# Local attention output transposed by DMA instead of TensorE, with the first layer's products issued one at a time

## The chip, the cores and the metric

The kernel runs on one core of one Trainium2 chip. The metric is the device time of one execution in microseconds (us). A core has TensorE (PE in the profile, with its weight loads as PEld), VectorE (DVE), ScalarE (ACT), GpSimd (POOL) and SyncE (SP); each works through its own instructions in the order in which the kernel issues them, and they wait for one another by semaphores. Loads are issued from POOL, stores and DMA transposes from SP.

## What is computed

Sparse attention over 8 batches, 8 heads, 576 positions and head dimension 64, and after it a two-layer perceptron on 4608 tokens (512 to 2048 to 512) with the Mish function between. Heads 0 to 3 are local (a position sees the 32 positions up to itself), heads 4 to 7 strided (it sees earlier positions that are congruent to it modulo 32).

```python
rel = pos[:, None] - pos[None, :]
mask_local = (rel >= 0) & (rel < stride)
mask_strided = (rel >= 0) & (pos[None, :] % stride == pos[:, None] % stride)
scores = np.where(masks, scale * q @ k.T, -1e9)
attn = softmax(scores)
x = (attn @ v).transpose(0, 2, 1, 3).reshape(B * S, H * D)
h = x @ w_in
g = h * np.tanh(np.log1p(np.exp(h)))     # Mish
out = g @ w_out
```

## The kernel before

**Blocks.** `run(plan, t)` (L712) is called for t = 1 to 8, after a hand-written start for the first tokens. Block t does three things at once: the first layer for tokens 512t to 512t+511 (`Mlp1(t)`), the second layer for the block before (`Mlp2(t - 1)`, from t = 2), and the attention of batch b = t + 1, as long as b < 8. So attention ends with t = 6; blocks 7 and 8 have none. After them the second layer of the last block remains.

**The layers.** Both are Strassen-like: seven products of half-size matrices in place of eight, with sums of operands formed by DVE ahead of them. In `Mlp1`, the 2048 columns of w_in are four quarter groups g = 0 to 3; each has products 1 to 7 of four matmuls each (`prod`, L386). Their results lie in three PSUM banks be, al and E (of two sets that take turns):

- step a (L411): product 5 into E, copy of E to s5, product 1 into al, copy of al to be by ACT;
- step b: product 6 onto al, copy of al to s2, product 3 onto E, DVE adds E and s2 into h, product 2 onto be;
- step c: product 7 onto al, DVE adds al and s5 into h; step d: product 4 onto al;
- steps U, W, H: Mish on ACT of be, al and h into gT.

The copies to s5 and s2 go to `self.eng`: ACT for t up to 6, DVE for t = 7 and 8. In `Mlp2`, "m" in a plan is one half of a product, eight matmuls (`half`, L470); there are 14. `x_sum` (x0 to x3) and `g_sum` (g1 to g3, and n for the next block) are the DVE sums of the operands; x0 reads the strided rows of xT, x1 to x3 the local ones (x_half, L366).

**Attention.** `qk` (q0 to q5) multiplies transposed q and k and takes the exponential on ACT into P_s and P_l; `mask` multiplies them with a mask, on POOL from t = 3 (in t = 2 the first four on DVE). Each "v" in a plan takes the next of a list: for batches 3 to 7 this is five `pv` of strided heads (s0 to s4), two `xt` of them, then two `pv` of local heads, an `xt`, two `pv`, an `xt`. A `pv` is a few matmuls into bank A0 or A1, a reciprocal and a product on DVE into x_s or x_l. An `xt` (L324) transposes x_s or x_l on PE into one of these banks and copies it into xT, the first layer's operand. xT is a ring of four batches.

**Queues.** "D" issues four DMA transposes of the next batch's raw k and q on SP (kTs, qTs, kTl, qTl; L188); SP also issues the stores of the output. "R" (L790) is on POOL: `hold` reads a corner of each of these four tiles, so that POOL waits until the transposes have landed; then it loads v of the next batch (L154, L157) and q and k of the batch after it (L137, L151). The masks are on POOL too. "s" spreads the loaded v on DVE.

**Order.** The plans are strings, written out, one token to a step; `SECOND` is for t = 1, `MAIN2` for t = 2, `MAIN` for t = 3 to 6 and `PLAIN` for t = 7 and 8. Their order is the order of issue on every engine.

Of the kernel before, what the change touches and what calls it, by code (L numbers as in the profile page):

```python
# [16 lines left out]
NW = 6  # L17
WQ = 96
# [3 lines left out]
RING = 4  # L22
# [23 lines left out]
def kernel(ctx, tc, q, k, v, moe_w_in, moe_w_out, out):  # L46
# [191 lines left out]
    class Attn:  # L238
# [54 lines left out]
        def pv(self, kind, n0, n1, bank, eng=None):  # L293
# [27 lines left out]
                in1=rden[0:m, 0:nu].unsqueeze(2).to_broadcast([m, nu, D]), op=ALU.mult,  # L321
            )

        def xt(self, kind, hf, bank, eng):  # L324
            tr = bank[:].bitcast(BF16)
            t0 = (self.b % RING) * S
            if kind == "l":
                for w in range(NW):
                    u = 12 * hf + 2 * w
                    PE.transpose(  # L330
                        tr[:, WQ * w:WQ * w + WQ], x_l[0:WQ, u:u + 2, :].rearrange("p u d -> p (u d)"),
                        ident[0:WQ, 0:WQ],
                    )
                cast(eng, xT[:, hf, t0:t0 + S], tr[:, 0:S])
            else:
                for j in range(CS):
                    u = 16 * hf + 2 * j
                    PE.transpose(  # L338
                        tr[:, PN * j:PN * j + PN], x_s[0:PN, u:u + 2, :].rearrange("p u d -> p (u d)"),
                        ident[0:PN, 0:PN],  # L340
                    )
                cast(
                    eng, xT[:, 2 + hf, t0:t0 + S].rearrange("p (n j) -> p n j", j=CS),
                    tr[:, 0:576].rearrange("p (j n) -> p n j", j=CS),
                )
# [35 lines left out]
    class Mlp1:  # L381
# [18 lines left out]
                    )  # L400

        def step(self, s, g):
            z = (self.t + g + 1) % 2
            be, al, E = [x[:] for x in SETS[z]]
            if self.eng is Dv:
                z = ((self.t + 1) % 2, 2, self.t % 2, (self.t + 1) % 2)[g]
                be, al, E = [x[:] for x in ((A1, A0, SETS[(self.t + 1) % 2][2]) if g == 1 else SETS[z])]
            h = hh[z]
            o = gT[:, 4 * g:4 * g + 4, :]
            two = lambda x: x.rearrange("p (u n) -> p u n", u=2)  # L410
            if s == "a":  # L411
                self.prod(5, g, E, True)
                cast(self.eng, s5[z][:], E)
                self.prod(1, g, al, True)
                Sc.copy(be, al)  # L415
            elif s == "b":
                self.prod(6, g, al, False)
                cast(self.eng, s2[z][:], al)
                self.prod(3, g, E, False)
                add(Dv, h[:, 0, :], E, s2[z][:])  # L420
                self.prod(2, g, be, False)
            elif s == "c":
                self.prod(7, g, al, False)
                add(Dv, h[:, 1, :], al, s5[z][:])
            elif s == "d":
                self.prod(4, g, al, False)
            elif s == "H":
                Sc.activation(  # L428
                    o[:, :, 256:512], h[:].rearrange("p i (u n) -> p (i u) n", u=2), AF.Mish
                )  # L430
            elif s == "U":
                Sc.activation(o[:, 0:2, 0:256], two(be), AF.Mish)
            elif s == "W":
                Sc.activation(o[:, 2:4, 0:256], two(al), AF.Mish)  # L434
# [130 lines left out]
    with tc.manual_schedule():  # L565
# [146 lines left out]
        def run(plan, t):  # L712
            b = t + 1
            m1, m2, nxt = Mlp1(t), Mlp2(t - 1), Mlp2(t)
            at = Attn(b) if b < B else None
            if b == B:
                unread(1, A1)
            ms = m2.steps() if t > 1 else []
            bank = [1, 0] if t == 1 else [0, 1]

            def v_steps():
                def pv(kind, r):
                    at.pv(kind, *r, (A0, A1)[bank[0]])
                    bank[0] = (bank[0] + bank[1]) % 2

                def xt(kind, hf):
                    at.xt(kind, hf, (A0, A1)[bank[0]], Sc if t == 1 and kind == "l" else Dv)
                    bank[0] = (bank[0] + bank[1]) % 2
                P = lambda kd, r: (lambda: pv(kd, r))
                X = lambda kd, hf: (lambda: xt(kd, hf))  # L730
                if t == 1:
                    return (
                        [P("l", r) for r in PV_L[:3]] + [X("l", 0), P("l", PV_L[3]), P("s", PV_S[0]), X("l", 1)]
                        + [P("s", r) for r in PV_S[1:]] + [X("s", 0), X("s", 1)]
                    )
                return (
                    [P("s", r) for r in PV_S] + [X("s", 0), X("s", 1)]
                    + [P("l", r) for r in PV_L[:2]] + [X("l", 0)]
                    + [P("l", r) for r in PV_L[2:]] + [X("l", 1)]
                )  # L740
            vs_ = late + (v_steps() if at else [])
            late.clear()
            JOBS = [("s", 0), ("s", 1), ("s", 2), ("l", 0), ("l", 1), ("l", 2)]
            for w in plan.split():
                c, n = w[0], int(w[1:]) if len(w) > 1 else 0
                if c in "abcdHUW":
                    m1.step(c, n)
                elif c == "p":
                    plain(t, n, deal1[n], act=False)
                elif c == "y":  # L750
                    Sc.activation(gT[:, n, :], deal1[n][:], AF.Mish)
                    if deal1[n] is A0:
                        bank[:] = [0, 1]
                elif c == "w":
                    w_out_sums(n, Dv)
                elif c == "m":
                    ms.pop(0)()
                elif c == "x":
                    x_sum(t, n, Dv)
                elif c == "g":  # L760
                    m2.g_sum(n, Dv)
                elif c == "n":
                    nxt.g_sum(0, Dv, 0, 8)
                elif not at:
                    continue
                elif c == "e":
                    Sc.preload_act_table(AF.Exp)
                elif c == "f":
                    Sc.preload_act_table(AF.Mish)
                elif c == "q":  # L770
                    at.qk(*JOBS[n], PAIRS[n % 2 * (1 + (t + 1) % 2)])
                    at.mask(*JOBS[n], Dv if t == 1 or t == 2 and n in (0, 1, 2, 3) else Po)
                elif c == "v":
                    if vs_:
                        vs_.pop(0)()
                elif c == "s":
                    spread_v(Dv)
                    if t > 1:
                        share_v(b, Dv)
                elif c == "h":  # L780
                    share_v(b, Dv)
                elif b + 1 >= B:
                    continue
                elif c == "t":
                    t_step(2, "l", "kq"[n // 2], n % 2, (C[1], C[2], A0, A1)[n], (Sc, Dv)[n % 2])
                    if n == 3:
                        load_qk(3)
                elif c == "D":
                    transpose_by_dma()
                elif c == "R":  # L790
                    hold(kTs, qTs, *((kTl, qTl) if t > 1 else ()))
                    load_vs(b + 1)
                    load_vl(b + 1)
                    if b + 2 < B:
                        load_qk(b + 2)
            assert not ms
            if t == 1:
                late.extend(vs_)
            else:
                for w in vs_:  # L800
                    w()

        late = []
        MAIN = (
            "x0 m m e m m x1 s x2 g1 g2 q0 q1 m m m m g3 q2 q3 m m q4 q5 m D v m f R a0 v v m m v v b0 a1 x3 c0 v "
            "U0 v b1 d0 U1 W0 c1 v a2 d1 W1 v H0 a3 v v b2 v H1 c2 b3 c3 d2 W2 v H3 d3 n U2 U3 W3 H2"
        )
        SECOND = (
            "t0 p0 q2 p1 t1 t2 t3 w1 p2 q3 w2 p3 q5 q4 p4 h p5 p6 f v y0 D y1 p7 s v p8 R y3 y6 v y2 v p9 v v y5 y4 "
            "p10 p11 y9 p12 y8 y7 y11 v v p13 v y13 p14 y10 p15 y14 n v y12 w3 y15"  # L810
        )
        MAIN2 = (
            "v m m v m e v x0 x1 m x2 g1 q1 q0 g2 m m m m g3 q2 s q3 m m q4 q5 m D f v m v a0 R v m m v v b0 a1 x3 "
            "c0 v v b1 d0 U0 U1 W0 c1 v a2 d1 W1 v H0 a3 v v b2 v c2 H1 b3 c3 d2 W2 v H3 d3 U2 U3 W3 H2 n"
        )
        PLAIN = (
            "m m x0 g1 x1 m m x2 x3 a0 m m g2 m b0 m m m g3 m m c0 U0 a1 H0 m m b1 d0 W0 a2 c1 a3 b2 b3 c3 d1 U2 H1 "
            "W1 U1 c2 d3 W3 U3 d2 H2 W2 H3 n"
        )

        for t in range(1, NBLK):
# [40 lines left out]
```

## Time and profile before

| | |
|---|---|
| median of 3 runs | 294.25 us (293.95 to 294.44) |
| the profiled execution | 294.54 us, of it 292.8 us in the span of the profile |
| granted TensorE clock | 0.999 of full speed |
| PE busy per block, t = 3 to 6 | 29.2 to 29.3 of 29.6 to 29.7 us |
| DVE, ACT, POOL busy in such a block (t = 4) | 22.6, 24.4, 17.5 us |
| PE busy, t = 7 | 25.1 of 25.2 us |
| x_l on PE in one block | 12 transposes |

The profile lists, per engine and group of equal instructions, the busy time, the mean duration and the idle time before them with the instruction that ended it. In the timeline, a line gives the start, the duration, the engine, the line of the kernel, the operation, what it writes and reads, and in brackets idle time of that engine just before. The chain of waits is followed back from the last instruction and names at each step what released it. Matmuls are pipelined: each is shown for about 0.27 us, and they start 0.11 us apart.

### The profile page before, as it was taken

Reading aid. Unit: us, or ns where it says so; the run is one execution under the profiler, and the core shown is the slowest. Engines: PE = TensorE matmul, PEld = TensorE weight load, DVE = VectorE, ACT = ScalarE, POOL = GpSimd, SP = SyncE. Lnnn points to the kernel's source line nnn. Section 1 sums busy time; section 2 is a strip of 40 time slices with the busy share of each in tenths; the row PEclk is TensorE's granted clock in tenths of the full one; section 3 lists DMA queues with packets and bytes.
Section 4 is the critical chain, followed back from the end, with each engine's and each line's share of the span. In section 5 each row is a group of like instructions: output and inputs, shape, how many; then the busy total and the mean of one; then the engine's idle time right before and its main releaser. Section 6 shows DMA issues by size and latency. Waiting matters only on the chain.

```text
span 292.8 us, 7799 instructions
## 1 busy us (share of the span) xinstructions
PE 282.4 (96%) x3256; PEld 223.8 (76%) x3268; DVE 205.7 (70%) x387; ACT 204.7 (70%) x361; POOL 102.7 (35%) x109
## 2 busy tenths in 40 slices
PE   8889999999999999999999999999999999999995
PEld 3564545545788888888888888888898888888884
DVE  2583548587798896688768866886688667757842
ACT  2578793769667789778977898789878526825650
POOL 8754330131614533981399039502920000000000
PEclk9999999999999999999999999999999999999999
DMA  7999999999999999999699989950110003003004
GB/s 136 179 204 202 203 194 185 174 169 150 137 154 181 204 174 70 165 223 166 32 167 215 167 39 147 231 36 2 72 73 2 2 29 118 1 3 143 2 0 143
DMA packets 94415, 35.84 MB, mean 122 GB/s; under 512 B 75804, under 2 KB 90124, under 8 KB 94380
## 3 DMA queue, kind: packets, MB, share of 16 engines
q0 software_dynamic: 61712, 18.71, 70.1%
q1 hardware_dynamic: 31708, 15.73, 24.4%
q10 hardware_dynamic: 960, 0.91, 1.0%
q8 instruction: 25, 0.41, 0.6%
q14 instruction: 10, 0.08, 0.1%
HBM read 37.87 MB, written 9.44 MB: 162 GB/s over the span
## 4 chain that ended last, share of the span: by engine, by line
PE 77%; ACT 8%; DVE 7%; issue 3%; DMA 3%; POOL 1%; ACTq 0%; POOLq 0%
PE al L129 34%; PE ee L129 19%; PE be L129 12%; PE at L129 5%; DVE hh L123 4%; PE at L310 3%; ACT s L118 3%; DMA vraw<-in_v_dram 3%; ACT gT L428 1%; PE at L338 1%; ACT Pl L281 1%; ACT gT L434 1%; DVE x_l L319 1%; ACT be L415 1%; PE at L330 1%
## 5 line engine op out<-in xcount | busy, mean ns | idle before, releaser
L129 PEld LDWEIGHTS <-w_in 128*128 128x128 bf16 x464 | 44.3, 98 | 20.6 <-issue 5.0
L129 PEld LDWEIGHTS <-gs 128*128 128x128 bf16 x512 | 48.7, 98 | 6.3 <-DVE gs L123 0.3
L129 PEld LDWEIGHTS <-wis 128*128 128x128 bf16 x472 | 44.5, 99 | 9.2 <-issue 3.2
L129 PEld LDWEIGHTS <-gT 128*128 128x128 bf16 x448 | 42.0, 98 | 10.0
L287 POOL TENSOR_TENSOR Ps<-Ps,consts_sb 72x864 bf16<-72x864 bf16 (+1 forms) x12 | 23.2, 1957 | 48.2 <-ACT Ps L281 48.2
L123 DVE TENSOR_TENSOR gs<-gT,gs 128x2048 bf16<-128x2048 bf16 x16 | 21.0, 1312 | 15.4 <-PE al L129 9.7
L129 PE MATMUL al<-wos,gs 128*128 128x256 bf16 x256 | 31.8, 273 | 0.0
L129 PE MATMUL al<-xs,wis 128*128 128x256 bf16 x208 | 30.4, 272 | 0.1
L428 ACT ACTIVATE gT<-hh 128x1024 bf16<-128x1024 f32 x26 | 27.7, 1067 | 0.0
L129 PE MATMUL al<-xT,w_in 128*128 128x256 bf16 (+1 forms) x141 | 25.8, 300 | 1.6 <-ACT gT L434 0.9
L129 PE MATMUL be<-xT,w_in 128*128 128x256 bf16 (+1 forms) x139 | 25.1, 299 | 0.2 <-issue 0.2
L287 POOL TENSOR_TENSOR Pl<-Pl,consts_sb 128x960 bf16<-128x960 bf16 (+1 forms) x14 | 22.2, 1608 | 7.6 <-ACT Pl L281 7.6
L129 PE MATMUL be<-w_out,gT 128*128 128x256 bf16 (+1 forms) x157 | 23.3, 293 | 0.2
L314 DVE RECIPROCAL rden<-at 96x6 f32<-96x6 f32 (+2 forms) x64 | 12.1, 189 | 14.6 <-PE at L310 10.8
L434 ACT ACTIVATE gT<-al 128x512 bf16<-128x512 f32 x26 | 15.6, 601 | 7.8 <-PE al L129 7.8
L319 DVE TENSOR_TENSOR x_s<-at,rden 72x448 bf16<-72x448 f32 (+1 forms) x34 | 19.9, 585 | 1.2
L123 DVE TENSOR_TENSOR hh<-al,s 128x512 f32<-128x512 f32 x26 | 17.8, 684 | 2.8 <-PE al L129 2.4
L123 DVE TENSOR_TENSOR hh<-ee,s 128x512 f32<-128x512 f32 x26 | 17.8, 684 | 2.5 <-ACT s L118 1.9
L123 DVE TENSOR_TENSOR gs<-gT 128x2048 bf16<-128x2048 bf16 x16 | 19.5, 1218 | 0.0
L129 PE MATMUL al<-w_out,gT 128*128 128x256 bf16 (+1 forms) x143 | 19.3, 284 | 0.1
L120 DVE COPY xT<-at 128x576 bf16<-128x576 bf16 x25 | 14.5, 597 | 4.5 <-PE at L330 4.3
L319 DVE TENSOR_TENSOR x_l<-at,rden 96x384 bf16<-96x384 f32 x30 | 16.6, 553 | 1.0
(185 smaller groups left out, 573.9 us busy)
## 6 DMA issues: line engine op xcount, KB each, us to landing
out_dram<-osb SPq DMA_DIRECT2D x16, 512.0 KB, 3.4
vraw<-in_v_dram POOLq DMA_DIRECT2D x8, 288.0 KB, 6.1
w_out<-in_moe_w_out_dram POOLq DMA_DIRECT2D x4, 512.0 KB, 15.4
ql<-in_q_dram POOLq DMA_DIRECT2D x7, 288.0 KB, 10.8
vl<-in_v_dram POOLq DMA_DIRECT2D x7, 288.0 KB, 9.1
kl<-in_k_dram POOLq DMA_DIRECT2D x5, 384.0 KB, 11.0
ks<-in_k_dram POOLq DMA_DIRECT2D x6, 288.0 KB, 8.2
qs<-in_q_dram POOLq DMA_DIRECT2D x6, 288.0 KB, 9.1
```

The source lines that it names most:

```text
L118: Sc.copy(out_, in_)
L120: eng.tensor_copy(out_, in_)
L123: eng.tensor_tensor(out=out_, in0=a, in1=b, op=op)
L129: PE.matmul(o, lhsT=lhsT, rhs=rhs, start=start, stop=stop, skip_group_check=True)
L281: Sc.activation(pt[0:n, e, 0:o], ps[e][0:n, 0:o], AF.Exp, scale=scale)
L287: meng.tensor_tensor(out=pm, in0=pm, in1=mk[0:n, :].unsqueeze(1).unsqueeze(1).to_broadcast([n, 2, nu, w]), op=ALU.mult,)
L310: PE.matmul(po[:, n - n0, :], lhsT=pt[0:r, c0:c0 + 128], rhs=rhs, start=True, stop=True)
L314: Dv.reciprocal(rden[0:m, 0:nu], po[0:m, :, D])
L319: Dv.tensor_tensor(out=x[0:m, n0:n1, :], in0=po[0:m, :, 0:D], in1=rden[0:m, 0:nu].unsqueeze(2).to_broadcast([m, nu, D]), op=ALU.mult,)
L330: PE.transpose(tr[:, WQ * w:WQ * w + WQ], x_l[0:WQ, u:u + 2, :].rearrange("p u d -> p (u d)"), ident[0:WQ, 0:WQ],)
L428: Sc.activation(o[:, :, 256:512], h[:].rearrange("p i (u n) -> p (i u) n", u=2), AF.Mish)
L434: Sc.activation(o[:, 2:4, 0:256], two(al), AF.Mish)
```

## The change

Local x of batches 3 to 7 is transposed by two DMA transposes on SP, `xt_by_dma`, each issued right behind the `pv` that completes its half of x_l; the transposes on PE and the copies on DVE for them are gone. "v" has 11 steps in place of 13. "R" is split: V holds on the four transposes and loads v, and R, now at the end of the block, holds on the second half of xT and then loads q and k. Steps a and b are split, so that each product is a step: a, i, b, j, k. A and B are a and b with the copy on the other of the two engines ACT and DVE. The four plans are written anew.

```diff
--- before.py
+++ after.py
@@ -321,6 +321,13 @@
                 in1=rden[0:m, 0:nu].unsqueeze(2).to_broadcast([m, nu, D]), op=ALU.mult,
             )
 
+        def xt_by_dma(self, hf):
+            t0 = (self.b % RING) * S
+            nc.sync.dma_start_transpose(
+                xT[:, hf, t0:t0 + S].rearrange("c (w n) -> c w n", w=NW),
+                x_l[0:WQ, 12 * hf:12 * hf + 12, :].rearrange("p u d -> p (u d)"),
+            )
+
         def xt(self, kind, hf, bank, eng):
             tr = bank[:].bitcast(BF16)
             t0 = (self.b % RING) * S
@@ -400,6 +407,9 @@
                     )
 
         def step(self, s, g):
+            eng = self.eng
+            if s in "AB":
+                s, eng = s.lower(), Dv if eng is Sc else Sc
             z = (self.t + g + 1) % 2
             be, al, E = [x[:] for x in SETS[z]]
             if self.eng is Dv:
@@ -410,14 +420,17 @@
             two = lambda x: x.rearrange("p (u n) -> p u n", u=2)
             if s == "a":
                 self.prod(5, g, E, True)
-                cast(self.eng, s5[z][:], E)
+                cast(eng, s5[z][:], E)
+            elif s == "i":
                 self.prod(1, g, al, True)
                 Sc.copy(be, al)
             elif s == "b":
                 self.prod(6, g, al, False)
-                cast(self.eng, s2[z][:], al)
+                cast(eng, s2[z][:], al)
+            elif s == "j":
                 self.prod(3, g, E, False)
                 add(Dv, h[:, 0, :], E, s2[z][:])
+            elif s == "k":
                 self.prod(2, g, be, False)
             elif s == "c":
                 self.prod(7, g, al, False)
@@ -726,6 +739,10 @@
                 def xt(kind, hf):
                     at.xt(kind, hf, (A0, A1)[bank[0]], Sc if t == 1 and kind == "l" else Dv)
                     bank[0] = (bank[0] + bank[1]) % 2
+
+                def last_l(hf):
+                    pv("l", PV_L[2 * hf + 1])
+                    at.xt_by_dma(hf)
                 P = lambda kd, r: (lambda: pv(kd, r))
                 X = lambda kd, hf: (lambda: xt(kd, hf))
                 if t == 1:
@@ -735,15 +752,14 @@
                     )
                 return (
                     [P("s", r) for r in PV_S] + [X("s", 0), X("s", 1)]
-                    + [P("l", r) for r in PV_L[:2]] + [X("l", 0)]
-                    + [P("l", r) for r in PV_L[2:]] + [X("l", 1)]
+                    + [w for hf in range(2) for w in (P("l", PV_L[2 * hf]), lambda hf=hf: last_l(hf))]
                 )
             vs_ = late + (v_steps() if at else [])
             late.clear()
             JOBS = [("s", 0), ("s", 1), ("s", 2), ("l", 0), ("l", 1), ("l", 2)]
             for w in plan.split():
                 c, n = w[0], int(w[1:]) if len(w) > 1 else 0
-                if c in "abcdHUW":
+                if c in "ABabcdijkHUW":
                     m1.step(c, n)
                 elif c == "p":
                     plain(t, n, deal1[n], act=False)
@@ -787,12 +803,14 @@
                         load_qk(3)
                 elif c == "D":
                     transpose_by_dma()
-                elif c == "R":
+                elif c == "V":
                     hold(kTs, qTs, *((kTl, qTl) if t > 1 else ()))
                     load_vs(b + 1)
                     load_vl(b + 1)
-                    if b + 2 < B:
-                        load_qk(b + 2)
+                elif c == "R" and b + 2 < B:
+                    if t > 1:
+                        hold(xT[:, 1, b % RING * S:])
+                    load_qk(b + 2)
             assert not ms
             if t == 1:
                 late.extend(vs_)
@@ -802,20 +820,22 @@
 
         late = []
         MAIN = (
-            "x0 m m e m m x1 s x2 g1 g2 q0 q1 m m m m g3 q2 q3 m m q4 q5 m D v m f R a0 v v m m v v b0 a1 x3 c0 v "
-            "U0 v b1 d0 U1 W0 c1 v a2 d1 W1 v H0 a3 v v b2 v H1 c2 b3 c3 d2 W2 v H3 d3 n U2 U3 W3 H2"
+            "m m g1 g2 m e m q0 q1 m s m m m q2 q3 g3 m m q4 q5 D m f x0 x1 v V x2 m v a0 v i0 m v m v b0 v a1 i1 j0 "
+            "k0 x3 c0 v b1 j1 d0 U0 c1 k1 W0 A2 U1 i2 v d1 v W1 H0 A3 i3 v v b2 j2 b3 k2 H1 c2 c3 k3 d2 n W2 H2 j3 U3 "
+            "U2 d3 H3 W3 R"
         )
         SECOND = (
-            "t0 p0 q2 p1 t1 t2 t3 w1 p2 q3 w2 p3 q5 q4 p4 h p5 p6 f v y0 D y1 p7 s v p8 R y3 y6 v y2 v p9 v v y5 y4 "
+            "t0 p0 q2 p1 t1 t2 t3 w1 p2 q3 w2 p3 q5 q4 p4 h p5 p6 f v y0 D y1 p7 s v p8 V R y3 y6 v y2 v p9 v v y5 y4 "
             "p10 p11 y9 p12 y8 y7 y11 v v p13 v y13 p14 y10 p15 y14 n v y12 w3 y15"
         )
         MAIN2 = (
-            "v m m v m e v x0 x1 m x2 g1 q1 q0 g2 m m m m g3 q2 s q3 m m q4 q5 m D f v m v a0 R v m m v v b0 a1 x3 "
-            "c0 v v b1 d0 U0 U1 W0 c1 v a2 d1 W1 v H0 a3 v v b2 v c2 H1 b3 c3 d2 W2 v H3 d3 U2 U3 W3 H2 n"
+            "v m m v m e v g1 m q1 g2 q0 s m m m m g3 x0 x1 q3 m q2 x2 m q5 q4 m v D f m v A0 v i0 m V v m v B0 x3 k0 "
+            "A1 i1 c0 v j0 v b1 j1 k1 d0 U0 W0 U1 c1 v a2 i2 d1 v W1 H0 A3 v i3 v b2 j2 k2 H1 c2 b3 j3 k3 c3 d2 d3 W2 "
+            "H3 U2 U3 H2 W3 n R"
         )
         PLAIN = (
-            "m m x0 g1 x1 m m x2 x3 a0 m m g2 m b0 m m m g3 m m c0 U0 a1 H0 m m b1 d0 W0 a2 c1 a3 b2 b3 c3 d1 U2 H1 "
-            "W1 U1 c2 d3 W3 U3 d2 H2 W2 H3 n"
+            "x0 m g1 m m g2 x1 m x2 a0 x3 m i0 m m B0 j0 m m g3 c0 m m m k0 A1 i1 m b1 U0 m d0 W0 j1 H0 a2 i2 c1 k1 "
+            "A3 i3 b2 j2 B3 j3 k3 c3 H1 k2 U1 c2 d1 U2 d3 W1 W3 n d2 H2 H3 W2 U3"
         )
 
         for t in range(1, NBLK):
```

## The prediction

> **What bounds the kernel now.** I read the page's busy shares first, then the block lengths from the timeline (where product 1 of the second layer starts: 107.76, 137.36, 166.95, 196.63, 226.44, 251.64, 276.83 us), then the timeline and the chain of waits inside one block.
>
> ```profile
> PE 282.4 (96%) x3256; PEld 223.8 (76%) x3268; DVE 205.7 (70%) x387; ACT 204.7 (70%) x361; POOL 102.7 (35%) x109
> ```
>
> PE is busy 96% of the span, so TensorE is the bound on average; blocks with attention (t = 3 to 6) take 29.6 to 29.8 us, the two without (t = 7, 8) 25.2 us. Time in a block is counted below from its product 1 (136.9 for t = 4). From the chain: 16 products of 256 columns stream in 1.75 us (0.109 each). A block has 224 of them, 24.5 us; qk adds about 1.34, the PV of strided heads 0.97 and of local heads 4 x 0.18, the transposes of x_s 0.52, those of x_l 0.52. That is 28.57 of 29.6: **0.52 us is local transposes and 1.03 us is loose**. The tail of the block shows both:
>
> ```profile
> 160.89 0.60 PE L129 MATMUL al<-xT,w_in 128*128 128x256 bf16 x4 [0.19 <-ACT gT L434]
> 161.32 0.42 PE L330 MATMUL at<-consts_sb,x_l 96*128 96x96 bf16 x6
> 161.58 0.35 PE L310 MATMUL at<-vl,Pl 128*128 128x65 bf16 x6
> ...
> 165.93 0.42 PE L330 MATMUL at<-consts_sb,x_l 96*128 96x96 bf16 x6
> 166.52 0.60 PE L129 MATMUL al<-xs,w_in 128*128 128x256 bf16 x4 [0.17 <-DVE hh L123]
> ```
>
> A group of six transposes holds PE from 161.32 to 161.58, 0.26 us. In brackets are PE's two marked gaps of the block: once it waits for ACT's Mish, once for DVE's addition. The chain of waits agrees: until 159.2 it is PE throughout, then it runs over ACT and DVE to the end of the block.
>
> ```profile
> 158.77 0.45 PE ee L129 x4
> ...
> 159.25 0.45 ACT s L118
> ...
> 160.24 0.59 ACT gT L434
> 160.84 0.70 ACT gT L428
> ...
> 165.19 1.29 DVE hh L123 x2
> ```
>
> From 159.2 to 166.5 (7.3 us) PE's own work is 13 products, 3 PVs and two transpose groups: 5.69 + 0.54 + 0.52 = 6.75. So this tail is shared by PE, ACT and DVE with only 0.55 us between them.
>
> **The change, part by part.**
>
> *Transposes gone from PE.* Two groups in each of five batches: 10 x 0.26 = 2.6 us of PE's queue, with no cover anywhere, since PE is the bound. Between 0 (if the tail is set by ACT and DVE alone) and 2.6; I take all of it, because the same edit relieves those two engines.
>
> *Casts gone from DVE.* Two copies of 0.46 (rows at 161.78 and 166.39) per batch. Nothing waits for them but the next block, so by themselves 0; they free DVE in the tail.
>
> *Casts moved between ACT and DVE.* In t = 3 to 6, A2 and A3 put two copies of E on DVE (0.68 busy) instead of ACT (0.58, spaced 0.475 when back to back). ACT gains 0.95 us in the tail, DVE takes 1.2 and lost 0.9. I walked the new order by hand with the spacing of the trace (product 0.4375, result 0.16 later; copies 0.475, H 0.94, additions 0.60, rden with x_l 0.70). Positions in the block: a0 at 12.6, b0 15.9, c0 18.3, d0 19.9, d1 22.3, b2 24.1, d2 27.2, d3 28.0, end 28.5. DVE's additions for c2 and c3 come out at 27.1 and 27.7, just ahead of d2 and d3; ACT's W1 at 23.35, about 0.1 after i3 wants its bank. ACT then has 3.2 us of Mish left for the next block; before, H ended 3.5 us in (139.41 + 1.07). So the loose 1.03 falls to some 0.6 (the changes between qk and products, about 0.1 each, stay). Bounds for this part, per block: gain 1.03 (nothing loose left), loss 0.9 (DVE works from 21.8 to the end without a pause; one addition of 0.68 and the spacing after it more in the way). I take 0.33 gained, near the walk.
>
> *t = 2.* The same 0.52; but A0, A1 and B0 also go to DVE, which is busiest there (26.25 of 29.7 us), 3 x 0.69 more against 0.92 less. I take 0.6 in all, with 0 and 1.4 as ends.
>
> *t = 7, 8.* No attention, so no transposes; only the order. 25.2 against 24.5 of products: 0.7 loose, of which one wait for DVE of 0.17 and 0.26. The new order puts d1 and d3 between c2 and d2, so that c2's addition (result 0.16, addition 0.68) has 0.875 us of cover. I take 0.2 per block; ends 0.6 gained, 0.5 lost.
>
> *Ten DMA transposes on SP's queue.* The nearest row is qTl, 96 rows and twice the columns:
>
> ```profile
> 151.31 1.59 SPq L197 DMA_TRANSPOSE qTl<-ql  x1
> ...
> 152.94 1.32 SPq L537 DMA_DIRECT2D out_dram<-osb  x2
> ```
>
> SP holds 1.27 to 1.79 us for one and it lands 3.7 to 7.2 us after issue, median 4.2. For half the data I take 1 and 3.5 (ends 0 and 7.2). Behind them on SP is only the next block's work. Their result is read by x1, x2 of the next block, which moved behind q5 to about 11 us: x_l is ready at 25.9, xT at 29.4, some 10 us early. PE pays 0.
>
> *Loads of q and k behind them.* This is the added wait: on POOL, the hold on xT sits ahead of four loads and these ahead of the next block's masks.
>
> ```profile
> 143.86 5.80 POOL L287 TENSOR_TENSOR Ps<-Ps,consts_sb 72x864 bf16<-72x864 bf16 x3 [11.37 <-ACT Ps L281]
> 149.63 4.83 POOL L287 TENSOR_TENSOR Pl<-Pl,consts_sb 128x960 bf16<-128x960 bf16 x3
> ...
> 157.67 0.73 POOL L137 DMA_DIRECT2D ks<-in_k_dram  x1
> 158.39 0.72 POOL L137 DMA_DIRECT2D qs<-in_q_dram  x1
> 159.10 1.46 POOL L151 DMA_DIRECT2D kl<-in_k_dram  x1
> 160.53 1.22 POOL L151 DMA_DIRECT2D ql<-in_q_dram  x1
> ```
>
> POOL spends 4.1 us on the four; 11.4 us idle ahead of the masks is the cover. With xT landed at 29.4 (0.9 into the next block) and 0.5 for the hold, they are out at 5.5; the first mask wants POOL at 6.5 to 7. Cost 0, with about 1 us in hand. It happens only ahead of t = 3, 4 and 5. The loads land 8 to 12 us after issue, so kTl's transposes start at some 13 us instead of 12 (148.95), the loads of v go out near 19 to 20 and land by 28; the spreading of v is wanted at 5 of the next block. Cost 0.
>
> **Sum**, against the profiled execution of 294.54 us (span 292.8): 4 blocks x (0.52 + 0.33) = 3.4; t = 2 0.6; t = 7, 8 0.4; together 4.4. All up to 77.4 us and the last block are unchanged. That gives 290.1; the median of the runs shown is 0.3 lower, 294.25, so **289.9 us** is the forecast for the median.
>
> **Rivals.**
>
> *Slower: the masks wait for the transposes.* If xT lands after about 30.4 (4.5 us after x_l), POOL's four loads push the masks, and PV s1, which the new order puts at 12.4 us and which needs the third mask (6.5 + 5.8 = 12.3), stops PE one for one. With an SP issue of 3.45 (qTs at 88.33, beside loads) and a landing of 7.2 it would be some 4 us late; half-way, 2.5 us in three blocks: 289.9 + 7.5 = 297.4. For it: v's loads may run beside these transposes, and PE has no slack at s1. Against: with the loads beside them the four transposes at 86.9 took 11.2 us to the last hold, without 9.6, and these are half as large. The Trainium skill, "VectorE: DVE Perf Modes", The three transpose paths and Rules for kernel authors, speaks against the edit: 1309 ns for a 128x128 by DMA, 390 ns on TensorE, which it prefers where PSUM will do; six tiles would be 7.9 us (an estimate from that page), and this rival. The traces bear it out poorly: qTl, twelve tiles, landed in 4.2 us at the median.
>
> *No change: the tail is set by ACT and DVE.* The chain's last 7 us speak for it: PE would wait where it transposed, and the moved casts only shift the queue to DVE. Then the tail stays 7.3 us, and what DVE loses in t = 2 takes what t = 7, 8 give: 292.5 to 294.9.
>
> *More than forecast.* Everything loose closes: 5 x 0.52 + 5 x 0.8 + 2 x 0.5 = 7.6, 286.7.
>
> **How the numbers follow.** Forecast 0.58 (287.9 to 291.8), more 0.05, no gain or little 0.20 (of it 0.08 faster by over 0.2%, 0.05 within, 0.07 slower), masks late 0.17. Within 0.2% (0.6 us) is about what a measurement of this kernel can't tell from no change. Faster 0.71, same 0.05, slower 0.24. The range 287.9 to 295.0 leaves out the 0.05 below and most of the late masks.
>
> **What would show it.** Right: blocks of t = 3 to 6 at 28.6 to 28.9 us, no x_l on PE, PE's waits for DVE and ACT in the tail no longer than now, POOL's first mask still near 7 us into the block, and xT's holds short. Wrong: a wait of PE's PV for POOL's mask at 12 us into t = 3 to 5; a wait of products j2, d2 or d3 for DVE; the holds on xT over 3 us into the next block; or blocks of t = 7, 8 over 25.2.

## The result, and the profile after

The changed kernel takes **319.75 us** (median of 4 runs, 319.2 to 322.1) against 294.35 (293.95 to 294.5): 1.088 times the time before, interval 1.083 to 1.094. The forecast was 289.9 us, the range 287.9 to 295.0. Ratios and intervals, here and below, leave out executions that took over 1.5% longer than the fastest of their kernel, while medians and ranges are of all of them. The profiled execution took 322.1 us, of it 320.3 in the span, with a mean granted clock of 0.957.

The busy row of the page, and the rows of PE and of the granted clock in 40 slices of the span (tenths):

```profile
PE 291.4 (91%) x3196; PEld 227.1 (71%) x3208; DVE 230.9 (72%) x381; ACT 203.8 (64%) x357; POOL 107.7 (34%) x112
...
PE   8999999999989993999769994999769999999995
...
PEclk9999999999999998799959998799968999999999
```

PE issued 60 instructions fewer and was yet busy 9 us longer; the clock shows why. There are four dips, one in each block with attention on POOL. Block lengths, from product 1 of one second layer to the next (us):

| block t | 2 | 3 | 4 | 5 | 6 | 7 | 8 |
|---|---|---|---|---|---|---|---|
| before | 30.31 | 29.60 | 29.59 | 29.68 | 29.81 | 25.20 | 25.19 |
| after | 31.28 | 36.93 | 35.55 | 36.51 | 37.26 | 24.94 | 24.94 |
| forecast | 29.7 | 28.6 to 28.9 | 28.6 to 28.9 | 28.6 to 28.9 | 28.6 to 28.9 | 25.0 | 25.0 |

Blocks 3 to 6 cost 27.6 us more, which is all of it (the span grew by 27.5; the other differences cancel). So one thing happens four times. In block 3, which starts at 108.37, PE's timeline (start, duration, then in brackets the idle time ahead) shows where:

```profile
120.73 0.40 PE L310 MATMUL at<-vs,Ps 72*128 72x65 bf16 x7
125.08 0.61 PE L129 MATMUL ee<-xs,wis 128*128 128x256 bf16 x4 [3.95 <-DVE xs L123]
126.90 0.54 PE L310 MATMUL at<-vs,Ps 72*128 72x65 bf16 x7 [1.21 <-DVE x_s L319]
127.25 1.04 PE L129 MATMUL al<-xT,w_in 128*128 128x256 bf16 x4
128.09 1.92 PE L129 MATMUL al<-w_out,gs 128*128 128x256 bf16 x8
```

Product 5 (step a0) waits 3.95 us for the operand sum in xs, then a PV waits for x_s; and then eight matmuls take 1.92 us where they took 1.04 at 119.86 in the same block. The table by stretches (length, then busy time and count of PE, PEld, DVE, ACT and POOL, the granted clock, DMA share and GB/s) has the clock:

```profile
120.70:125.10 4.40, 0.45 (x10) 0.32 (x9) 4.37 (x2) 0.92 (x1) 4.40 (x4) 1.00 1.31 157
125.10:133.50 8.40, 7.19 (x58) 5.54 (x59) 5.74 (x14) 2.71 (x5) 3.48 (x7) 0.59 0.81 170
```

```profile
126.80:128.60 1.80, 1.70 (x14) 1.32 (x14) 1.77 (x6) 0.21 (x1) 0.18 (x1) 0.50 0.89 164
...
132.30:134.20 1.90, 1.90 (x24) 1.65 (x22) 1.36 (x3) 1.47 (x3) 0.00 (x0) 0.90 1.19 156
```

Over the 8.4 us from 125.1, behind the gap, the clock is 0.59 on the mean; if it is 0.50 or 1.00 at any time, that is half speed for some 6.9 us. Of PE's 7.19 busy us there 0.41, 2.9 us, are lost (an estimate). So block 3 pays 3.95 + 1.21 + 2.9 = 8.1 us; on top of the 28.85 that such a block takes without this (the x-early kernel, below) that makes 36.9, and 36.93 was measured.

Why is the sum late? DVE's and POOL's timelines of the same stretch:

```profile
116.22 1.71 DVE L123 TENSOR_TENSOR gs<-gT,gs 128x2048 bf16<-128x2048 bf16 x1 [1.05 <-ACT Ps L281]
118.52 0.69 DVE L123 TENSOR_TENSOR osb<-ee,o 128x512 f32<-128x512 f32 x1 [0.59 <-PE ee L129]
119.13 5.90 DVE L123 TENSOR_TENSOR xs<-xT 128x512 bf16<-128x512 bf16 x1
125.06 1.02 DVE L123 TENSOR_TENSOR xs<-xT,xs 128x512 bf16<-128x512 bf16 x1
```

```profile
109.86 0.18 POOL L180 COPY hold<-xT 32x1 bf16<-32x1 bf16 x1 [7.24 <-DMA xT<-x_l]
...
113.28 1.60 POOL L151 DMA_DIRECT2D ql<-in_q_dram  x1
114.90 5.95 POOL L287 TENSOR_TENSOR Ps<-Ps,consts_sb 72x864 bf16<-72x864 bf16 x3
120.80 5.00 POOL L287 TENSOR_TENSOR Pl<-Pl,consts_sb 128x960 bf16<-128x960 bf16 x3
```

x0, the first xs line, wasn't waiting for its data: DVE has no idle time ahead of it. It is shown as *busy* for 5.90 us, for what took 0.42 before. It stands there through the end of the second mask and all of the third, fourth and fifth (single starts 119.57, 120.80, 122.75), and ends 0.3 us into the sixth (124.71). The addition into osb just ahead of it, which reads one of its operands from PSUM, took its usual 0.69 us in the middle of the second mask. In the kernel before, the same instruction stood here, with POOL doing no masks until 143.86:

```profile
138.30 0.42 DVE L123 TENSOR_TENSOR xs<-xT 128x512 bf16<-128x512 bf16 x1
138.75 0.42 DVE L123 TENSOR_TENSOR xs<-xT,xs 128x512 bf16<-128x512 bf16 x1
```

The list of an operand's instructions tells it in one figure (min/median/max in ns): before, no xs took over 426; after, the longest took 5901. In each of blocks 3 to 6 x0 took 5.83 to 5.90 us, and PE waited 3.90 to 3.96 for it. The chain of waits names only "DVE xs L123 8%", and the list of waits has PE waiting for DVE's xs (15.7 us, four times) but no DVE waiting for POOL, because to the profile DVE is working.

```profile
L123 DVE TENSOR_TENSOR xs<-xT x14: 418/420/426, 81.6 to 256.0; 128x512 bf16<-128x512 bf16 x14
```

```profile
L123 DVE TENSOR_TENSOR xs<-xT x14: 409/418/5901, 87.9 to 284.0; 128x512 bf16<-128x512 bf16 x14
```

The parts that the forecast spoke of look as it said. The tail of block 3 in the chain of waits is PE with a single link of ACT, where before it ran over ACT and DVE for 7 us; SP issues both transposes in 3.17 us, and the hold lets go at 145.8, 0.5 us into the next block:

```profile
138.94 0.45 PE al L129 x4
...
139.42 0.61 ACT gT L447
...
140.07 0.60 PE al L129 x4
```

```profile
140.48 3.17 SPq L326 DMA_TRANSPOSE xT<-x_l  x2
```

### The profile page after: what moved, and what is told of

It is laid out like the page before. It is cut to its first block, busy times and chain, and to the rows that moved or that the text cites. A ratio compares the mean times of both kernels' runs of the same rounds, so it can differ in the third digit from the quotient of the medians.

```text
span 320.3 us, 7689 instructions
## 1 busy us (share of the span) xinstructions
PE 291.4 (91%) x3196; PEld 227.1 (71%) x3208; DVE 230.9 (72%) x381; ACT 203.8 (64%) x357; POOL 107.7 (34%) x112
## 4 chain that ended last, share of the span: by engine, by line
PE 81%; DVE 11%; ACT 4%; issue 3%; DVEq 0%; ACTq 0%
PE al L129 36%; PE ee L129 19%; PE be L129 14%; DVE xs L123 8%; PE at L129 4%; PE at L310 3%; DVE x_s L319 1%; ACT Pl L281 1%; ACT gT L447 1%; PE at L345 1%; PE at L337 0%; DVE osb L123 0%; DVE rden L314 0%; DVE hh L123 0%; PE ee L224 0%
## 5 line engine op out<-in xcount | busy, mean ns | idle before, releaser
L129 PEld LDWEIGHTS <-gs 128*128 128x128 bf16 x512 | 51.7, 103 | 8.5
L123 DVE TENSOR_TENSOR gs<-gT,gs 128x2048 bf16<-128x2048 bf16 x16 | 21.4, 1336 | 18.6 <-ACT gT L441 10.7
L129 PE MATMUL ee<-xs,wis 128*128 128x256 bf16 x112 | 17.7, 283 | 15.7 <-DVE xs L123 15.7
L129 PE MATMUL al<-xs,wis 128*128 128x256 bf16 x208 | 31.1, 276 | 0.0
L129 PE MATMUL al<-xT,w_in 128*128 128x256 bf16 (+1 forms) x141 | 27.6, 316 | 0.9 <-ACT Pl L281 0.2
L123 DVE TENSOR_TENSOR xs<-xT 128x512 bf16<-128x512 bf16 x14 | 27.6, 1971 | 0.0
L287 POOL TENSOR_TENSOR Pl<-Pl,consts_sb 128x960 bf16<-128x960 bf16 (+1 forms) x14 | 23.8, 1725 | 2.3 <-ACT Pl L281 2.3
L426 ACT COPY be<-al 128x512 f32<-128x512 f32 x26 | 15.1, 580 | 14.3 <-PE al L129 14.3
L123 DVE TENSOR_TENSOR hh<-ee,s 128x512 f32<-128x512 f32 x26 | 17.7, 685 | 7.0 <-ACT s L118 4.3
L129 PE MATMUL al<-w_out,gs 128*128 128x256 bf16 x128 | 22.5, 337 | 0.0
L118 ACT COPY s<-al 128x512 f32<-128x512 f32 x23 | 13.5, 587 | 13.6 <-PE al L129 13.4
L310 PEld LDWEIGHTS <-Ps 72*128 72x128 bf16 x256 | 14.3, 106 | 9.4 <-issue 6.1
```

What stands on the lines that cost most here:

```text
L118: Sc.copy(out_, in_)
L123: eng.tensor_tensor(out=out_, in0=a, in1=b, op=op)
L129: PE.matmul(o, lhsT=lhsT, rhs=rhs, start=start, stop=stop, skip_group_check=True)
L287: meng.tensor_tensor(out=pm, in0=pm, in1=mk[0:n, :].unsqueeze(1).unsqueeze(1).to_broadcast([n, 2, nu, w]), op=ALU.mult,)
L310: PE.matmul(po[:, n - n0, :], lhsT=pt[0:r, c0:c0 + 128], rhs=rhs, start=True, stop=True)
```

## The experiments

**Theories.** There are three. M: x0, x1, x2, moved from the start of the block into POOL's run of masks, are shut out by POOL, and the gap that this makes in PE's work halves the clock. D: the DMA transposes (their traffic, or the hold that puts POOL's loads and masks later) cause it. O: it is the casts moved to DVE and the split steps. Each kernel was compared with the kernel before.

**The kernel before, with x0, x1, x2 late.** Nothing else of the change is in it.

```diff
-"x0 m m e m m x1 s x2 g1 g2 q0 q1 m m m m g3 q2 q3 m m q4 q5 m D v m f R a0 v v m m v v b0 a1 x3 c0 v "
+"m m e m m s g1 g2 q0 q1 m m m m g3 q2 q3 m m q4 q5 m x0 x1 x2 D v m f R a0 v v m m v v b0 a1 x3 c0 v "
```

> The kernel before with one edit: in MAIN the sums x0, x1, x2 stand behind q5 and the eleventh half product, in the middle of POOL's masks; local transposes stay on TensorE. Theory M: x0 takes 4 to 6 us there too, PE waits some 4 us ahead of product 5 and its clock drops behind it; 4 blocks x 6 to 8 us, in all 318 to 326 us. Rivals D and O: no DMA transpose of x and no moved copy here, so within 2 us of 294.3.

325.31 us, ratio 1.096 (1.088 to 1.104). Blocks 3 to 6: 36.28, 36.93, 35.57, 36.75. DVE's, POOL's and PE's lines of block 3:

```profile
121.10 5.67 DVE L123 TENSOR_TENSOR xs<-xT 128x512 bf16<-128x512 bf16 x1
```

```profile
116.78 5.81 POOL L287 TENSOR_TENSOR Ps<-Ps,consts_sb 72x864 bf16<-72x864 bf16 x3 [7.02 <-ACT Ps L281]
122.55 4.99 POOL L287 TENSOR_TENSOR Pl<-Pl,consts_sb 128x960 bf16<-128x960 bf16 x3
```

```profile
126.83 1.03 PE L129 MATMUL ee<-xs,wis 128*128 128x256 bf16 x4 [3.97 <-DVE xs L123]
```

Without a DMA transpose of x, a hold on it or a moved cast, the whole loss is there. M holds; D and O are not needed for it.

**The changed kernel, with x0, x1, x2 early.** The mirror image.

```diff
-"m m g1 g2 m e m q0 q1 m s m m m q2 q3 g3 m m q4 q5 D m f x0 x1 v V x2 m v a0 v i0 m v m v b0 v a1 i1 j0 "
+"x0 m m g1 x1 x2 g2 m e m q0 q1 m s m m m q2 q3 g3 m m q4 q5 D m f v V m v a0 v i0 m v m v b0 v a1 i1 j0 "
```

> The changed kernel with one edit: in MAIN (t = 3 to 6) the sums x0, x1, x2 stand in the first 2 us of the block, before any mask, instead of behind q5. Theory M (a DVE sum with both operands in SBUF cannot run while POOL's masks, which read SBUF too, are in progress): x0 falls from 5.9 to 0.42 us, PE's wait of 3.95 and the slow clock behind it go, blocks of t = 3 to 6 take 28.4 to 28.9 us, in all 289 to 292 us. Rival D (x0 is slow because of the DMA transposes and what they wrote): xT is read sooner behind its transposes, so x1 and x2 stay slow or get slower and the time stays over 310. Rival O (DVE is overloaded by the moved copies): the stall moves to the tail, 300 to 310.

299.59 us, ratio 1.014 (1.007 to 1.021). Blocks 30.13, **38.31**, 28.85, 28.85, 29.06, 24.94, 24.94: blocks 4 to 6 are within 0.2 us of the forecast's 28.6 to 28.9, and block 3 is longer than in the changed kernel. There another DVE instruction was shut out, the copy that spreads v; DVE's, POOL's and PE's lines:

```profile
113.22 1.67 DVE L120 COPY vs<-vraw 72x2048 bf16<-72x2048 bf16 x1
114.91 9.87 DVE L120 COPY vl<-vl 32x1280 bf16<-32x1280 bf16 x1
```

```profile
110.41 1.13 POOL L180 COPY hold<-xT 32x1 bf16<-32x1 bf16 x1 [7.44 <-DMA xT<-x_l]
...
115.70 4.83 POOL L287 TENSOR_TENSOR Ps<-Ps,consts_sb 72x864 bf16<-72x864 bf16 x3
120.49 5.06 POOL L287 TENSOR_TENSOR Pl<-Pl,consts_sb 128x960 bf16<-128x960 bf16 x3
```

```profile
128.05 0.54 PE L310 MATMUL at<-vs,Ps 72*128 72x65 bf16 x7 [6.80 <-DVE x_s L319]
```

The hold let POOL go only 4.0 us into this block (107.52 to 111.54), so its loads ran straight into the masks, at 115.70, with no pause; in block 4 of the same run there were 2.06 us between them, and the same copies took 0.68 and 0.48. So D has a part after all: where the transposes land late, the exclusion reaches other instructions. (The kernel below without DMA transposes of x and without the hold bears this out: its block 3 takes 29.64.)

**x0, x1, x2 right behind g3.** In the changed kernel g3 got in after the first mask (1.71 us at 116.22, where 1.22 is usual); does what follows it at once get in as well?

```diff
-"m m g1 g2 m e m q0 q1 m s m m m q2 q3 g3 m m q4 q5 D m f x0 x1 v V x2 m v a0 v i0 m v m v b0 v a1 i1 j0 "
+"m m g1 g2 m e m q0 q1 m s m m m q2 q3 g3 x0 x1 x2 m m q4 q5 D m f v V m v a0 v i0 m v m v b0 v a1 i1 j0 "
```

> The changed kernel with x0, x1, x2 moved only by two half products, to stand right behind the sum g3, still inside the masks. Theory M, with the port going to whoever has it until it lets go: g3 gets in at the end of the first mask (it waited 0.5 us), and x0 to x2 follow it without a gap and keep POOL out for 1.2 us more; x0 0.42 us, PE's wait gone or under 1 us, 289 to 294 us in all. If instead each sum must queue anew behind all masks that are ready, x0 again takes 4 to 6 us and the time stays at 315 to 325.

324.42 us, ratio 1.102 (1.097 to 1.108). It doesn't: x0 took up to 7.18 us, so each DVE instruction stands in line anew.

**A pause behind each mask.** A copy of 32x1 on POOL that reads what the mask just wrote, so that POOL can't start the next mask until this one has landed.

```diff
                     at.mask(*JOBS[n], Dv if t == 1 or t == 2 and n in (0, 1, 2, 3) else Po)
+                    if t > 2:
+                        hold(flat((P_s, P_l)[n // 3][n % 3][:]))
```

> The changed kernel with one edit: behind each of POOL's masks (t = 3 to 6) stands a 32x1 copy on POOL that reads what the mask wrote, so that POOL has to wait for its own mask before it can go on. The sums stay where the change put them. Theory M2 (a DVE sum waits not for one mask but for the whole run of masks that POOL has ready, and gets in only where POOL has nothing ready behind the next instruction; all of x0's and g3's waits so far fit this): x0 now gets in at the end of the mask that is running, 0.4 to 2.5 us instead of 5.9, PE waits under 1 us, the clock stays up; 290 to 297 us. If a DVE sum is simply slow beside masks, or locked out until the last of them whatever lies between, x0 stays at 5 to 7 us and the time at 318 to 326.

300.80 us, ratio 1.023 (1.018 to 1.028). The same sums in the same place, in block 4, with the masks around them:

```profile
152.98 0.82 DVE L123 TENSOR_TENSOR xs<-xT 128x512 bf16<-128x512 bf16 x1
153.84 1.51 DVE L123 TENSOR_TENSOR xs<-xT,xs 128x512 bf16<-128x512 bf16 x1
```

```profile
151.71 1.81 POOL L287 TENSOR_TENSOR Ps<-Ps,consts_sb 72x864 bf16<-72x864 bf16 x1
153.59 0.26 POOL L180 COPY hold<-Ps 32x1 bf16<-32x1 bf16 x1
153.81 1.26 POOL L287 TENSOR_TENSOR Ps<-Ps,consts_sb 72x576 bf16<-72x576 bf16 x1
```

x0 now gets in at the pause at 153.59. So it isn't the masks' work that keeps DVE out (it is all still there) but that POOL has the next one ready. The gain is smaller than was expected: each sum still waits for one mask, and blocks 4 to 6 take 31.0 to 31.3. Block 3 takes 32.77, and there the clock fell to half for some 3.4 us, behind waits of PE of only 0.31, 0.38 and 1.30 us; in block 4, waits of 0.22, 0.38 and 1.30 left it at 1.00.

```profile
125.90:129.40 3.50, 3.50 (x27) 2.69 (x26) 1.97 (x5) 0.10 (x1) 2.65 (x7) 0.51 1.18 252
```

**All masks of t = 3 to 6 on DVE.**

```diff
-at.mask(*JOBS[n], Dv if t == 1 or t == 2 and n in (0, 1, 2, 3) else Po)
+at.mask(*JOBS[n], Po if t == 2 and n > 3 else Dv)
```

> The changed kernel with all masks of t = 3 to 6 on DVE instead of POOL, 0.65 us each by t = 2's rows instead of 1.3 to 2.3 on POOL. Theory M: nothing on POOL meets x0 any more, x0 takes 0.42 us; DVE gets 3.3 us more to do in the first half of the block, where it has pauses; blocks 28.4 to 29.4 us, 289 to 294 us in all. Theory D (transposes): x0 stays slow, over 310.

298.31 us, ratio 1.012 (1.011 to 1.014); the sums take 0.41 to 0.42 and blocks 4 to 6 are 30.7 to 30.9. (The profiled execution took 304.92; its block 2, at 34.69, is the longest seen.) With POOL away the exclusion is gone; but DVE is now the late one, and PE waits 0.81 us for x0 and 0.61 for x_s behind the masks. That cost wasn't in the expectation.

**PE kept busy through the wait.** 18 matmuls of 512 columns whose result nobody reads, ahead of a0 in t = 3 to 6.

```diff
+                if c == "Z":
+                    unread(n, SETS[(t + 1) % 2][2])
...
-... D m f x0 x1 v V x2 m v a0 v ...
+... D m f x0 x1 v V x2 m v Z18 a0 v ...
```

> The changed kernel with 18 matmuls of 512 columns (3.8 us) issued ahead of product 5 of a0 in t = 3 to 6, into a bank that this product then overwrites; their results are not used. They run while TensorE would wait for x0. If the slow clock behind the wait (0.5 for some 6 us, about 3.3 us of work lost per block) is due to the idle time itself, the clock stays at 1.0 and the blocks become about 3 us shorter, 306 to 310 us in all. If it comes from something else, the time stays within 2 us of 319.8.

314.93 us, ratio 1.070 (1.063 to 1.076); x0 still took 5.84, and in blocks 4 to 6 step a0 came as late as in the changed kernel, 16.6 to 16.7 us into the block (12.8 in the x-early kernel), now with PE busy up to it. The clock stayed at 1.00:

```profile
159.83:168.23 8.40, 7.05 (x86) 6.11 (x86) 7.50 (x17) 3.88 (x7) 3.44 (x7) 1.00 0.68 140
```

From a0 to their end these blocks took 17.74, 17.73 and 17.95 us, against 18.91, 19.87 and 20.55 in the changed kernel and 16.1 to 16.3 with x early. So the slow clock is made by the gap, and filling it is worth 1.2 to 2.6 us a block. PE's wait for x_s behind a0 was 1.22 to 1.23 in these blocks, and 0.78, 0.79 and 1.21 in the changed kernel's; with these taken off, the slow clock costs 1.6 to 2.6. About 3 was expected. Block 3 took 36.27 us for another reason: there g3 stood for 10.18, the longest of all, and PE was idle 1.92 us behind the unread matmuls, with the clock still at 1.00.

```profile
114.76 10.18 DVE L123 TENSOR_TENSOR gs<-gT,gs 128x2048 bf16<-128x2048 bf16 x1 [0.58 <-ACT Ps L281]
```

**x early, and local x transposed by PE again.** No hold on xT; the plans get one more v for each transpose (not shown below); the rest of the change stays.

```diff
-+ [w for hf in range(2) for w in (P("l", PV_L[2 * hf]), lambda hf=hf: last_l(hf))]
++ [P("l", r) for r in PV_L[:2]] + [X("l", 0)]
++ [P("l", r) for r in PV_L[2:]] + [X("l", 1)]
...
-                    if t > 1:
-                        hold(xT[:, 1, b % RING * S:])
```

> The kernel of the run with early sums, but with local x transposed on TensorE again (12 transposes and two copies per batch) and no hold on xT; order and step split stay those of the change. This gives the price of the DMA part alone. If the transposes were worth their TensorE time, blocks of t = 4 to 6 are 0.52 us longer than with DMA (28.85), 29.3 to 29.5 us; the stall of t = 3, which I put down to the late hold on xT, is gone; 291.5 to 294 us in all. If the tail was set by ACT and DVE, the blocks stay within 0.2 us of 28.85.

295.64 us, ratio 1.004 (1.001 to 1.006). Blocks 3 to 6: 29.64, 29.50, 29.50, 29.72; block 2, at 32.24, makes the whole longer than expected. Against the x-early kernel that prices the DMA transposes alone: 29.50 - 28.85 = 0.65 us a block. But 0.38 of it is a wait of PE for x_l at this placing of its transposes, so a better placing might leave as little as 0.27. Against before (29.59, 29.68, 29.81) the other edits give 0.1 to 0.2.

**x early, and q and k of t = 2 loaded ahead of xT's transposes.** An attempt on block 3: R right behind V in t = 2, without the hold.

```diff
-                    if t > 1:
+                    if t > 2:
                         hold(xT[:, 1, b % RING * S:])
...
-... D f m v A0 v i0 m V v m v B0 x3 k0 "
+... D f m v A0 v i0 m V R v m v B0 x3 k0 "
...
-            "H3 U2 U3 H2 W3 n R"
+            "H3 U2 U3 H2 W3 n"
```

> The kernel of the run with early sums, and in t = 2 alone R stands right behind V, without the hold on xT, so that POOL has issued its loads before t = 3 begins. Theory M: the 9.9 us that the spreading copy of v waited in t = 3 behind POOL's loads and masks go; t = 3 takes 28.8 to 29.3 us like t = 4 to 6, in all 288.5 to 291 us, faster than the kernel before. Rival: the loads now run beside the DMA transposes of x, these land 3 us later, x1 and x2 of t = 3 wait for them and the stall comes back in another place, 295 to 300.

300.31 us, ratio 1.022 (1.016 to 1.028). The loads then run beside the transposes, and xT lands about 11 us after x_l, where 3.5 was estimated; x1 waits for it, and x2 is shut out:

```profile
114.74 0.89 DVE L123 TENSOR_TENSOR xs<-xT,xs 128x512 bf16<-128x512 bf16 x1 [3.75 <-DMA xT<-x_l]
115.56 7.17 DVE L123 TENSOR_TENSOR xs<-xT 128x512 bf16<-128x512 bf16 x1
```

Block 3 takes 38.63. So at this place the loads do need the hold ahead of them, as the change has it.

**x early, and block 3 (or all blocks) relieved.** Four versions: the pauses of above in t = 3 to 6, or in t = 3 alone; the first four masks on DVE in t = 3 alone, or in t = 3 to 6. The first two lines below are alternatives, and so are the last two.

```diff
+                    if t > 2:
+                    if t == 3:
+                        hold(flat((P_s, P_l)[n // 3][n % 3][:]))
...
+at.mask(*JOBS[n], Dv if t == 1 or t in (2, 3) and n in (0, 1, 2, 3) else Po)
+at.mask(*JOBS[n], Dv if t == 1 or n in (0, 1, 2, 3) else Po)
```

> The kernel of the run with early sums, and in t = 3 to 6 a 32x1 copy on POOL behind each mask that reads what it wrote. Theory M2: no DVE operation waits longer than one mask and one copy (2.5 us); no round near 300; but the chain of masks grows by six waits of about 0.2 us, and TensorE waits for the third mask ahead of its second PV by 0.2 to 1 us in each block: 290 to 294 us.

> The kernel of the run with early sums, and in t = 3 alone a 32x1 copy on POOL behind each mask that reads what it wrote. Theory M2 (a DVE operation on the shared port gets in only where POOL has nothing ready behind its next instruction): the spreading copy of v that waited 9.9 us in t = 3 gets in behind the first mask at the latest, 1 to 3 us; t = 3 takes 29 to 31.5 us instead of 38.3, the others stay at 28.85; 288.5 to 292 us, faster than the kernel before. If the wait of t = 3 has another cause, 297 to 301 us as without the copies.

> The kernel of the run with early sums, and in t = 3 the first four masks on DVE, as t = 2 has them; POOL keeps two. Theory M2: POOL has nothing ready behind its last load until the local exponentials are through, so the spreading copy of v waits at most for one load, under 1.5 us; t = 3 takes 28.9 to 30.5 us; 288.5 to 291.5 us. If the late loads on POOL as such hold TensorE up in t = 3, over 295.

> The kernel of the run with early sums, and in t = 3 to 6 the first four masks on DVE, so that POOL keeps two per block. Theory M2: POOL never has a run of six masks ready behind its loads, so none of the lock-outs that cost single blocks 8 to 10 us in the runs before can happen; every block of t = 3 to 6 takes 28.7 to 29.3 us in every round, 288.5 to 291.5 us with a small spread, faster than the kernel before. If lock-outs come from something else than the run of masks, some rounds are again near 300.

| | median (range), us | ratio and interval | blocks 2 to 6, profiled |
|---|---|---|---|
| pauses, t = 3 to 6 | 295.51 (291.73 to 298.37) | 0.999 (0.995 to 1.002) | 33.2, 29.14, 29.22, 29.22, 29.43 |
| pauses, t = 3 | 294.04 (290.66 to 301.15) | 0.994 (0.991 to 0.998) | 31.17, 29.90, 37.33, 28.86, 29.06 |
| four masks on DVE, t = 3 | 295.72 (289.65 to 301.56) | 0.986 (0.983 to 0.988) | 29.99, 28.78, 28.85, 28.86, 29.07 |
| four masks on DVE, t = 3 to 6 | 293.0 (290.74 to 298.1) | 0.992 (0.989 to 0.996) | 29.99, 28.78, 29.15, 28.90, 30.01 |

The medians of the kernel before beside them were 294.6, 294.52, 294.52 and 294.6, and all four kernels came out above what was expected of them. The profile of the third shows what the forecast had in mind: 290.84 us, every block within 0.3 of what was written. But its four runs came at 289.7, 290.8, 300.6 and 301.6, so over all of them it gains nothing; the long ones have no trace, and that a DVE instruction was shut out beside POOL's masks in them is likely, not shown. In the second that can be seen: block 3 came through and block 4 didn't, where xT had landed 4 us into the block.

```profile
142.54 0.18 POOL L180 COPY hold<-xT 32x1 bf16<-32x1 bf16 x1 [7.60 <-DMA xT<-x_l]
```

```profile
145.14 2.52 DVE L120 COPY vl<-vl 32x1280 bf16<-32x1280 bf16 x1
147.69 9.64 DVE L123 TENSOR_TENSOR gs<-gT,gs 128x2048 bf16<-128x2048 bf16 x1
```

The fourth has the lowest median, 0.5% below the kernel before (0.8% by the ratio); its runs still spread over 7 us.

## Why the prediction was wrong

**The step that failed** is a half sentence in the part on the DMA transposes: the result "is read by x1, x2 of the next block, which moved behind q5 to about 11 us ... PE pays 0". x0, which moved with them, isn't mentioned. The move was looked at for one thing, whether the data are there. They were, long before. What DVE would meet at the new place was in view: POOL's six masks, copied into the prediction itself, at 143.86 to 154.46 in block 4, where 11 us into the block is 148. A hint of its price stood in the trace, too: g3, a DVE sum that already had its place beside the masks, took 1.60 us in blocks 4 to 6, where 1.22 is usual.

```profile
145.15 1.60 DVE L123 TENSOR_TENSOR gs<-gT,gs 128x2048 bf16<-128x2048 bf16 x1 [2.14 <-PE al L129]
```

The three sums went at cost 0 from a stretch where POOL held or loaded into one where it ran masks back to back. They cost 6.7 to 8.2 us a block (35.55 to 37.26 against 28.85 to 29.06).

**A second price was missing.** The rival with a long wait of PE priced it "one for one". A wait of some 3.9 us cost 1.6 to 2.9 more in the clock behind it (2.9 by the clock in block 3, 1.6 to 2.6 by the unread matmuls in blocks 4 to 6). Had the lock-out been foreseen, about 4 x (3.95 + 1.0 - 0.75) = 16.8 us would have been written for 27.6.

**Right in kind and near in size.** With x early, blocks 4 to 6 fell by 0.74 to 0.83 us where 0.85 was forecast: 0.65 for the transposes against their placing on PE above (0.52 forecast; between 0.27 and 0.65, as said there) and 0.1 to 0.2 for the rest (0.33). The rival by which ACT and DVE set the tail is thereby out. Blocks 7 and 8 gave 0.25 to 0.26 each (0.2). In block 3 the hold on xT began 2.7 and was done 3.4 us after the last x_l (142.43, 145.12, 145.82), where 3.5 and 0.5 for the hold were forecast.

**Block 2** (0.6 forecast) shows the same exclusion on a smaller scale. Its code is the same in ten of these kernels. It took 29.99 us in four of them and 30.13 in a fifth, where before has 30.31, and there no copy and no mask on DVE in it is longer than usual. It took 31.17, 31.28, 31.33, 33.2 and 34.7 in the other five; in each of these a copy of v on DVE took 1.05 to 1.38 us (0.48 or 0.68 is usual) beside POOL's load of ql, which had waited for a DMA transpose, and DVE's mask of 72x576 took 1.17 or 2.25 (0.45 is usual) beside POOL's masks. The changed kernel's, 31.28, is one of them:

```profile
85.67 1.05 DVE L120 COPY vl<-vl 32x1280 bf16<-32x1280 bf16 x1
...
89.26 1.17 DVE L287 TENSOR_TENSOR Ps<-Ps,consts_sb 72x576 bf16<-72x576 bf16 x1
```

PE then waited 1.03 us for x_s there, and in the 33.2 also 1.82 for that mask. So the 0.6 came out as 0.2 to 0.3 where nothing was shut out.

**The rival "the masks wait for the transposes"** came true in part ahead of block 3. The hold on xT began 4.8 us after the last x_l in the changed kernel and 6.2 in the x-early one, beyond the rival's 4.5; it let go 1.7 and 4.0 us into the block (forecast 1.4), and the masks began 6.5 and 8.2 us into it (forecast 6.5 to 7). In two of the last four kernels the hold began as late as 7.0 and 7.8 us after the last x_l, ahead of block 4; why the landing varies wasn't tried. By itself that cost PE nothing in the changed kernel and 0.39 us for a mask in the x-early one. What it did was to close the pause between POOL's loads and masks, and so to shut out more of DVE.

**The signs written down** were the wrong ones for this: in the changed kernel no PV waited for a mask at 12 us, and the waits for j2, d2 and d3 stayed small. "Blocks of 28.6 to 28.9" was the one that told.

## What to carry to other kernels

When a DVE instruction moves that reads two operands from SBUF or copies from SBUF to SBUF, read POOL's timeline at its new place as well as its data's: behind a run of POOL instructions that are all ready it can stand for the whole run, and it shows as busy, so look for one operation whose longest duration is many times its median. A wait of TensorE of some 4 us must be priced with the slow clock behind it, here 1.6 to 2.9 us more. Where something waits for a DMA transpose, look at what POOL loads beside it: in the one kernel that tried this, the pair of transposes took 11 us instead of some 3 to 8.

## What the runs showed of the hardware

**POOL keeps DVE out for more than one instruction.** The Trainium skill, "SBUF — State Buffer", Who interferes with whom, says that DVE with two inputs in SBUF and GpSimd share a port as an exclusive lock, held for the whole instruction by the one that issues first. The kind agrees: x0 stood while POOL ran masks, and the sums were at 0.41 to 0.42 us with the masks on DVE. By that rule x0 at 119.13 would have waited for the mask in progress, until 119.6; it waited through three more, 5.5 us, and here the measurement decides. Seen were 5.7 to 5.9 (x0), 7.2 (x0, x2), 9.6 and 10.2 (g3) and 9.9 us (a copy); with a pause behind each mask 0.8 to 1.6 for the sums x0 to x2 and at most 3.0 (a copy). A reading that fits nearly all of them is that DVE is let in where POOL has nothing ready behind the instruction that it is about to run. g3 got in at the boundary to the second mask when the third's exponentials weren't done, and the long ones all got in at POOL's last ready mask, behind which the semaphores of the trace have a hold wait for POOL's own result. One case does not fit: the copy at 145.14 above got in after 2.5 us though masks were ready behind the load. So the exact rule stays open. It works both ways: the second mask at 116.81 took 2.79 us, behind g3, where such a mask otherwise takes 1.8 to 1.95, and the hold at 110.41 in the x-early kernel took 1.13 us, beside a DVE sum, where 0.18 is the shortest.

**The clock after a gap.** In the changed kernel and the two others with x0, x1, x2 among the masks and PE idle behind them, PE waited 3.9 to 4.0 us for the sums twelve times; each time the clock then fell to 0.50, for some 7 us (once 3.4). With unread matmuls in the gap it stayed at 1.00. The Trainium skill, "TensorE: Matmul & The Clock Gate", Why this matters for your kernels, asks for no idle gaps over some 3 us, and these twelve agree. Shorter waits went both ways: 1.9 us left the clock at 1.00 (block 3 with the unread matmuls); 1.83 and 1.03 us close together in block 2 brought 0.50 for 3.4 us in one execution and left it at 1.00 in another; and 0.31, 0.38 and 1.30 brought it in the kernel with pauses. So a wait under 3 us isn't safe by itself, and what decides stays open.
